# Weight copies and weight sums placed at other points of an attention and mixer kernel on one Trainium2 core, and one weight piece converted elsewhere

## The chip, the core and the metric

The kernel runs on one core of a Trainium2 chip. The metric is device time in microseconds, the median of the runs shown. Names of engines: PE (TensorE, matmuls; PEld its weight loads), DVE (VectorE), ACT (ScalarE), POOL (GpSimd), SP (SyncE, which here issues nearly all DMAs, in order).

## What is computed

Windowed attention over 8 batches, 8 heads, 576 positions and head size 64, and then a mixer block. From the reference:

```python
scores = scale * np.matmul(q, k.transpose(0, 1, 3, 2))
mask = (rel >= 0) & (rel < 64)                      # rel = query position - key position
attn = softmax(np.where(mask, scores, -1e9))
x = (attn @ v) as (batch 8, seq 576, channels 512)
xt = x.transpose(0, 2, 1)
h = np.maximum(xt @ w_tok1, 0.0) @ w_tok2           # (576, 256), (256, 576)
u = x + h.transpose(0, 2, 1)
h2 = np.maximum(u @ w_ch1, 0.0) @ w_ch2             # (512, 1536), (1536, 512)
out = u + h2
```

The activations are float32, the four weights float64.

## The kernel before

**Precision.** Each float32 operand of a large product is split into two parts, `hi` (ACT's copy) and `lo` (the difference, by DVE or POOL), and a product is three matmuls: hi with hi, hi with lo, lo with hi. The float64 weights arrive as pairs of 32-bit words. Turning 384 columns of them into float32 is a *job*. `to_f32_a` (L195 to L198) and `to_f32_b` (L207 to L212) are six operations on DVE, with the last addition on POOL during attention; for *late* jobs ACT makes the absolute value (L185) and DVE adds. Jobs 0 to 6 are the token weights, 7 to 22 are `w_ch1` (kept in SBUF as `w1hi`, `w1lo`), 23 to 38 are `w_ch2` (`w2hi`, `w2lo`).

**Attention.** 36 tiles of 128 query rows, numbered `i`. In a tile, PE transposes the softmax, forms the output `xp`, the scores two tiles ahead, and the token product `h`; in spare places it also makes pieces of `u`, which are stored to `u_dram`. `JOBS[i]` says how many jobs tile `i` converts: one, except that tiles from 6 on whose number divides by 3 convert none. A job that is converted in one tile is finished in the next: a `w1` job is split (ACT, POOL), a `w2` job is stored to `w2_dram`, since the memory of `w2hi` and `w2lo` is not free yet. `N_FIRST` = 27 jobs are done here, four of them `w2`.

**The channel product** runs over nine chunks of 512 tokens. Chunk 0 is done whole: 12 pieces `gemm1` (L620, 12 matmuls each, into `gp`), each followed by `relu_split` (L607 on ACT gives `ghi`, L608 on DVE gives `glo`), and then four `gemm2` (L628, 36 matmuls each, `op_0` to `op_3`), each followed by `add_out` (L633 on DVE, L635 the store). Beside chunk 0 run the late jobs (`late_steps`, two steps a piece), and the four `w2` jobs that had been stored are read back 512 columns at a time (`load_w2`, L571, tile `raww2`) and split (`split_w2`, L104). `op_0` needs columns 0 to 1535 of `w2`, `op_1` the next 1536, and so on. A `raw` tile has three buffers, so the load of a late job on SP waits until DVE has done the L210 of the third job before it.

Chunks 1 and 2 are done in halves: 6 pieces of `gemm1`, then four `gemm2` of 18 matmuls. Chunks 3 to 8 are done in pairs by a scheme with seven products (`m1` to `m7`) for eight, which needs sums and differences of blocks of `w1`. These are prepared during chunk 1. `weight_steps` is a generator: it copies the blocks that need no sum to DRAM (`w1s`), 12 DMAs, and then makes four rounds of four steps, each with sums on DVE (L689 to L711), a split (`keep`, L101 on ACT and L104 on DVE, tiles `whi` and `wlo` with four buffers each), and two stores by `store_w1`. Chunk 1 takes two steps per piece. During chunk 2, SP begins to load the blocks from `w1s` into the place of `w1hi` and `w1lo`.

**Order.** The order of instructions on each engine is the order in which the program writes them (the schedule is manual). Every engine takes its own in order; semaphores tie them together. SP waits in order too: a DMA whose condition isn't met holds all that are behind it.

Of the kernel before, what the change touches and what calls it, by code (L numbers as in the profile page):

```python
# [10 lines left out]
F32 = mybir.dt.float32  # L11
# [10 lines left out]
C = H * D  # L22
P = 128
# [7 lines left out]
NCT = C // P  # L31
# [5 lines left out]

LAST_PARTS = 2

N_FIRST = 27  # L40


JOBS = {i: 1 if i < 6 or i % 3 else 0 for i in range(-1, 37)}
PIECES = {32: (1, 0), 33: (1, 0), 34: (1, 0), 35: (3, 0), 36: (2, 1)}

TOK1_FROM, TOK1_SLOW, TOK2_FROM = 2, 4, 7
# [8 lines left out]
NH = NFT // 2  # L55
PRODUCTS = ("m1", "m6", "m7", "m5", "m2", "m4", "m3")
# [27 lines left out]
def mixer_kernel(ctx: ExitStack, tc: tile.TileContext, qh, kh, vh, wt1, wt2, wc1, wc2, out):  # L84
    nc = tc.nc
# [7 lines left out]
    w1hi = const.tile([P, NCT * F], F32R, name="w1hi")  # L93
    w1lo = const.tile([P, NCT * F], F32R, name="w1lo")
    w2_dram = dram.tile([P, NFT * C], F32, name="w2_dram")
    w1s = [dram.tile([P, NH, NPROD, 2, P], F32, name=f"w1s{k}") for k in range(2)]
    u_dram = [dram.tile([P, NCT, CHUNK], F32, name=f"u_dram{j}") for j in range(NCHUNK)]

    def split(eng_hi, eng_lo, hi, lo, src):
        if eng_hi is nc.scalar:  # L100
            nc.scalar.copy(hi, src)  # L101
        else:
            eng_hi.tensor_copy(hi, src)
        eng_lo.tensor_sub(lo, src, hi.bitcast(F32))  # L104
# [18 lines left out]
    with ExitStack() as actx:  # L123
# [92 lines left out]
        jobs = [(wt1, t1hi, t1lo, o, 320) for o in range(0, 5 * DT, 320)]  # L216
        jobs += [(wt2, t2hi, t2lo, o, CW) for o in range(0, NTT * S, CW)]
        jobs += [(wc1, w1hi, w1lo, o, CW) for o in range(0, NCT * F, CW)]
        jobs += [(wc2, None, None, o, CW) for o in range(0, NFT * C, CW)]
        to_load, to_convert, to_finish = list(range(N_FIRST)), [], []  # L220

# [10 lines left out]
        def job_convert_a():  # L232
            if to_convert:
                n, raw = to_convert.pop(0)
                to_convert_b.append((n, to_f32_a(raw, jobs[n][4], n, n >= N_FIRST)))

# [5 lines left out]
        finished = set()  # L242

        def job_finish():
            if to_finish:
# [5 lines left out]
                else:  # L251
                    eng = nc.vector if src is wt2 or n >= N_FIRST else nc.gpsimd
                    split(nc.scalar, eng, hi[:, o:o + m], lo[:, o:o + m], w)
# [212 lines left out]
        tok1_plan, n = {}, 0  # L466
        for i in range(TOK1_FROM, NT + 1):
            m = min(n + (1 if i < TOK1_SLOW else 2), i)
            tok1_plan[i] = range(n, m)
            n = m  # L470
        qk(0)
        for i in range(-1, NT + 1):
# [6 lines left out]
            store_u()  # L479
            n_jobs = JOBS[i]  # L480
            if i == NT - 1:
# [67 lines left out]
    with ExitStack() as bctx:  # L549
# [11 lines left out]
        tctx = ExitStack()  # L561
        pl = tctx.enter_context(tc.tile_pool(name="pl", bufs=1))
        cpool[0] = pl
        first = [(o, C) for o in range(0, jobs[N_FIRST][3], C)]
        w2_raw = []

        def load_w2():
# [6 lines left out]
        def split_w2():  # L574
            if w2_raw:
                o, m, raw = w2_raw.pop(0)
                split(nc.scalar, nc.vector, w2hf[:, o:o + m], w2lf[:, o:o + m], raw[:, :m])

        to_load += range(N_FIRST, len(jobs))
        for n in to_load:  # L580
# [51 lines left out]
        def add_out(j, uf, ct, op, final, cols=slice(0, CHUNK)):  # L632
            nc.vector.tensor_add(uf[:, ct, cols], op, uf[:, ct, cols])  # L633
            if final:
                nc.sync.dma_start(out[j, :, ct, cols], uf[:, ct, cols])  # L635
# [5 lines left out]
            return ps.tile([P, CHUNK], F32, name=f"op{name}_{ct}", tag=tag, bufs=bufs)  # L641


        u = ul.pop(0)
        for ft in range(NFT):
            gemm1(0, ft, u, gbuf[ft])
            for _ in range(2):
                next(late, None)
            if ft in (1, 2, 7):
                load_w2()  # L650
            if ft in (6, 8, 10):
                split_w2()
            if ft == 3:
                ul[1] = load_u(1, pu)
            if ft == 8:
                split_u(ul[1])
        for ct in range(NCT):
            for _ in range(7):
                next(late, None)
            assert all(n in finished for n in range(23 + 4 * ct, 27 + 4 * ct))  # L660
            op = new_op("0", ct)
            gemm2(op, ct, range(NFT), gbuf, True, True)
            add_out(0, u[0], ct, op, True)
        tctx.close()


        pw = tctx.enter_context(tc.tile_pool(name="pw", bufs=1, reuse_waits="tile"))

        def store_w1(m, k, f0, ct, src):

            nf = src.shape[1] // P
            nc.sync.dma_start(w1s[k][:, f0:f0 + nf, PRODUCTS.index(m), ct],  # L672
                              src.bitcast(F32).rearrange("p (f c) -> p f c", c=P))

        def weight_steps():
            for m, half, ct0 in (("m1", 0, 0), ("m2", 0, 2), ("m4", 1, 2)):
                for ct in range(2):
                    for k, w in enumerate((w1hi, w1lo)):
                        o = (half * NCT + ct0 + ct) * NH * P
                        store_w1(m, k, 0, ct, w[:, o:o + NH * P])  # L680
            yield
            nf = CW // P
            for n in range(2 * NH // nf):
                ct, f0 = n % 2, n // 2 * nf

                def whole(tag, half, ct):
                    o = (half * NCT + ct) * NH * P + f0 * P
                    t = pw.tile([P, CW], F32, name=f"{tag}_{n}", tag=tag, bufs=1)
                    nc.vector.tensor_add(t, w1hi[:, o:o + CW].bitcast(F32), w1lo[:, o:o + CW].bitcast(F32))  # L689
                    return t  # L690

                def keep(m, x):
                    hi, lo = (pw.tile([P, CW], F32R, name=f"w{k}_{m}_{n}", tag=f"w{k}", bufs=4) for k in ("hi", "lo"))
                    split(nc.scalar, nc.vector, hi, lo, x)
                    for k, t in enumerate((hi, lo)):
                        store_w1(m, k, f0, ct, t)

                a = whole("wa", 1, ct)
                s1 = whole("ws", 1, 2 + ct)
                yield  # L700
                nc.vector.tensor_add(s1, s1, a)
                c = whole("wb", 0, ct)
                keep("m5", s1)
                yield
                nc.vector.tensor_sub(a, c, a)
                nc.vector.tensor_sub(c, s1, c)
                keep("m7", a)
                keep("m6", c)
                yield
                d = whole("wd", 0, 2 + ct)  # L710
                nc.vector.tensor_sub(d, d, c)  # L711
                keep("m3", d)
                yield
# [40 lines left out]


        steps = weight_steps()
        for j in range(1, N_PLAIN):
            u, last = ul.pop(j), j == N_PLAIN - 1
            if last:
                tctx.close()  # L760
                px.append(bctx.enter_context(tc.tile_pool(name="px", bufs=1, reuse_waits="tile")))
                load_raw(0, 0)
            for half in range(2):
                g = []
                for ft in range(half * NH, (half + 1) * NH):
                    g.append(new_g(f"{j}_{ft}"))
                    gemm1(j, ft, u, g[-1])
                    if j == 1:
                        for _ in range(2):
                            next(steps, None)  # L770
                    if not last and ft == 3:
                        ul[j + 1] = load_u(j + 1, pu)
                    if not last and ft == 8:
                        split_u(ul[j + 1])
                    if last:
                        if ft == 1:
                            sums()
                            prep(0, "m1", 0)
                            prep(0, "m6", 0)
                        if ft == 2:  # L780
                            prep(0, "m7", 0)
                            prep(0, "m5", 0)
                            prep(0, "m2", 0)
                            load_raw(0, 1)
                        if ft == 6:
                            load_w1(0)
                            sums()
                        if ft in (7, 8):
                            for m in (("m1", "m6"), ("m7", "m5", "m2"))[ft - 7]:
                                prep(0, m, 1)  # L790
                        if ft == 9:
                            sum4()
                if last and half == 1:
                    for m in ("m4", "m3"):
                        prep(0, m, 1)
                    load_raw(0, 0)
                    load_w1(1)
                    load_w1(2)
                for ct in range(NCT):
                    op = new_op(f"{j}_{half}", ct)  # L800
                    gemm2(op, ct, range(half * NH, (half + 1) * NH), g, True, True)
                    add_out(j, u[0], ct, op, half == 1)
                    if last and half == 1 and ct == 1:
                        sums(False)
                        sum4()
                        for m in ("m4", "m3"):
                            prep(0, m, 0)
# [132 lines left out]
```

## Time and profile before

| | |
|---|---|
| median of 3 runs | 866.21 us (866.21 to 866.83) |
| the profiled execution | 867.31 us, of which its span is 865.5 us |
| PE busy | 828.6 us, 96% of the span |
| DVE busy | 527.3 us, 61% |
| ACT busy | 336.4 us, 39% |
| POOL busy | 104.8 us, 12%, in attention alone |
| DMA | 136.11 MB, mean 157 GB/s |

The stages in the profiled execution: attention to about 283 us, chunk 0 to 350.7, chunk 1 to 427.6, chunk 2 to 492.9, the three pairs to the end. PE is the engine to look at: where it is busy all the time at full clock, another engine's work costs nothing. So a stage is read by its length beside what its matmuls need.

### The profile page before, as it was taken

The page shows a single profiled execution, that of the slowest core. Times are in us where ns is not written, and L with a number is a line of the kernel's source. Part 1 is how long each engine was busy: PE and PEld are TensorE (multiplying, and loading weights), DVE is VectorE, ACT ScalarE, POOL GpSimd, SP SyncE. Part 2 cuts the span into 40 slices and gives each one's busy share as a digit, 9 for nine tenths or more (in the row PEclk, how much of TensorE's full clock was granted, in tenths as well). Part 3 has the DMA queues.
Part 4 walks back from the last instruction along what each step waited for, and adds up shares of the span by engine and source line. Part 5 has one row for each costly group of instructions (what it writes and reads, how often), then busy time and mean ns, then how long its engine had stood idle before and what let it go on. Part 6 is the DMA issues. An engine that isn't in the chain of part 4 may idle for free.

```text
span 865.5 us, 14815 instructions
## 1 busy us (share of the span) xinstructions
PE 828.6 (96%) x5864; PEld 680.8 (79%) x5864; DVE 527.3 (61%) x939; ACT 336.4 (39%) x1018; POOL 104.8 (12%) x109
## 2 busy tenths in 40 slices
PE   6889999989989999969999999999999999999998
PEld 4668878868879878848888888887888888888886
DVE  4989878878885598555244443447735367635252
ACT  4778778778786351122022120213211123202020
POOL 3533343333332000000000000000000000000000
PEclk9999999999999999979999999999999999999999
DMA  9657676666644542792240751606361424542002
GB/s 323 201 189 250 191 247 220 217 210 232 207 153 132 161 141 85 204 275 82 87 154 1 267 200 69 219 1 218 109 256 60 159 86 135 182 182 86 1 0 98
DMA packets 71334, 136.11 MB, mean 157 GB/s; under 512 B 7008, under 2 KB 41568, under 8 KB 69344
## 3 DMA queue, kind: packets, MB, share of 16 engines
q1 hardware_dynamic: 69152, 133.32, 45.9%
q10 hardware_dynamic: 2112, 1.84, 0.6%
q8 instruction: 46, 0.75, 0.4%
q14 instruction: 24, 0.20, 0.1%
HBM read 104.46 MB, written 30.67 MB: 156 GB/s over the span
## 4 chain that ended last, share of the span: by engine, by line
PE 77%; DVE 10%; ACT 4%; SPq 2%; issue 2%; POOL 2%; DMA 2%; POOLq 0%; DVEq 0%; ACTq 0%
PE gp L839 18%; PE op L628 11%; PE gp L620 6%; PE h L368 5%; PE up L410 4%; PE s L276 4%; PE op_4a L628 4%; PE op_2b L628 4%; PE op_2a L628 4%; PE op_0b L628 4%; PE op_0a L628 4%; PE op_4b L628 4%; PE xp L323 3%; PE up L403 2%; SPq L672 2%
## 5 line engine op out<-in xcount | busy, mean ns | idle before, releaser
L839 PE MATMUL gp<-m,w1hi 128*128 128x512 f32 x504 | 155.4, 389 | 0.7 <-DVE x L847 0.7
L839 PEld LDWEIGHTS gp<-m,w1hi 128*128 128x128 f32 x504 | 94.5, 188 | 20.9 <-DVE x L847 1.5
L839 PE MATMUL gp<-m,w1lo 128*128 128x512 f32 x252 | 98.0, 389 | 0.0
L304 ACT ACTIVATE e<-e,nm 128x128 f32<-128x128 f32 x232 | 90.4, 396 | 8.2 <-DVE nm L296 8.2
L607 ACT ACTIVATE ghi<-x 128x512 fp32r<-128x512 f32 x54 | 34.1, 632 | 119.9 <-DVE x L849 68.3
L843 ACT COPY x<-gp 128x512 f32<-128x512 f32 x18 | 10.4, 578 | 143.8 <-PE gp L839 143.8
L607 ACT ACTIVATE ghi<-gp 128x512 fp32r<-128x512 f32 x50 | 29.6, 595 | 82.7 <-PE gp L620 82.5
L608 DVE SCALAR_TENSOR_TENSOR glo<-x,ghi 128x512 fp32r<-128x512 f32 x54 | 37.4, 693 | 38.1 <-ACT ghi L607 38.1
L628 PE MATMUL op<-ghi,w2hi 128*128 128x512 f32 x128 | 51.4, 401 | 6.0 <-ACT ghi L607 6.0
L620 PE MATMUL gp<-ulo,w1hi 128*128 128x512 f32 x144 | 56.0, 389 | 0.0
L620 PE MATMUL gp<-uhi,w1hi 128*128 128x512 f32 x144 | 56.0, 389 | 0.0
L620 PE MATMUL gp<-uhi,w1lo 128*128 128x512 f32 x144 | 56.0, 389 | 0.0
L839 PEld LDWEIGHTS gp<-m,w1lo 128*128 128x128 f32 x252 | 47.3, 188 | 9.9
L628 PE MATMUL op<-glo,w2hi 128*128 128x512 f32 x128 | 51.3, 401 | 0.9 <-DVE glo L608 0.8
L628 PE MATMUL op<-ghi,w2lo 128*128 128x512 f32 x128 | 51.0, 398 | 0.0
L104 POOL TENSOR_TENSOR xlo<-x,xhi 128x512 fp32r<-128x512 f32 x32 | 42.6, 1332 | 65.2 <-ACT xhi L101 64.8
L323 PEld LDWEIGHTS xp<-v,pt 128*64 128x64 f32 x1152 | 37.4, 137 | 16.5 <-ACT pt L313 6.2
L608 DVE SCALAR_TENSOR_TENSOR glo<-gp,ghi 128x512 fp32r<-128x512 f32 x50 | 34.2, 686 | 25.8 <-ACT ghi L607 25.7
L276 PE MATMUL s<-k,q 64*64 64x128 f32 x1152 | 43.4, 287 | 3.4 <-DVE c L207 1.9
L323 PE MATMUL xp<-v,pt 128*64 128x64 f32 x1152 | 43.2, 226 | 2.6 <-ACT pt L313 2.2
L304 ACT ACTIVATION_READ_ACCUMULATOR e<-e,nm 128x1 f32 x232 | 44.7, 193 | 0.0
L313 ACT COPY pt<-pp 128x512 f32<-128x512 f32 x72 | 41.9, 586 | 6.6 <-PE pp L311 6.4
(165 smaller groups left out, 1894.6 us busy)
## 6 DMA issues: line engine op xcount, KB each, us to landing
v<-vh SPq DMA_DIRECT2D x36, 512.0 KB, 3.7
w1hi<-w1s SPq DMA_DIRECT2D x18, 896.0 KB, 4.8
w1lo<-w1s SPq DMA_DIRECT2D x18, 896.0 KB, 6.6
raw<-wc SPq DMA_DIRECT2D x32, 384.0 KB, 4.4
q<-qh SPq DMA_DIRECT2D x36, 256.0 KB, 4.5
k<-kh SPq DMA_DIRECT2D x7, 1280.0 KB, 7.6
out<-uf SPq DMA_DIRECT2D x35, 256.0 KB, 2.6
uf<-u_dram SPq DMA_DIRECT2D x8, 1024.0 KB, 8.7
```

The costliest lines, as they stand in the source:

```text
L104: eng_lo.tensor_sub(lo, src, hi.bitcast(F32))
L276: nc.tensor.matmul(s[u][half * BLK:(half + 1) * BLK, j], qt[r, j, half], kbs[b][r, j, n * BLK:n * BLK + P], start=not on_pe, stop=True, sk ...
L304: nc.scalar.activation(e[:, h], src[:, h], AF.Exp, bias=nm[:, g:g + 1], scale=by, accum_out=sm[:, g:g + 1])
L313: nc.scalar.copy(pt, pp)
L323: nc.tensor.matmul(xp[half * BLK:(half + 1) * BLK, h], pts[h % 2][:, h // 2, half * BLK:(half + 1) * BLK], vt[:, half, h], start=True, sto ...
L368: nc.tensor.matmul(h_ps[b][tt], w[:, o + tt * P:o + (tt + 1) * P], x, start=first and n == 0, stop=last and n == len(combos) - 1)
L410: nc.tensor.matmul(up[:, :n], hx[:, cs], w[:, tt * S + s0:tt * S + s0 + n], start=False, stop=(k == 6), skip_group_check=True)
L607: nc.scalar.activation(hi, src, AF.Relu)
L608: nc.vector.scalar_tensor_tensor(out=lo, in0=src, scalar=0.0, in1=hi.bitcast(F32), op0=ALU.max, op1=ALU.subtract)
L620: nc.tensor.matmul(gp, w[:, w1_at(ft, ct)], x[:, ct], start=(k == 0), stop=(k == 3 * NCT - 1))
L628: nc.tensor.matmul(op, w[:, ct, ft], x[:, cols], start=(first and k == 0), stop=(last and k == 3 * len(gs) - 1), skip_group_check=not (fir ...
L839: nc.tensor.matmul(b, w[:, at], c[:, h, t], start=(n < 4 and k == 0), stop=(k == 5), skip_group_check=True)
```

## The change

It does three things.

- `N_FIRST` is 28 and tile 21 converts a job as well. The jobs from 17 on move one place ahead among the converting tiles, a fifth `w2` job (number 27) is stored to `w2_dram`, and eleven late jobs are left. A fourth `load_w2` (384 columns) and a fourth `split_w2` read it back beside chunk 0, and the splits stand behind pieces 6, 8, 9 and 11 instead of 6, 8 and 10.
- The 12 copies of blocks of `w1` leave `weight_steps`. Three of them follow each `gemm2` and its `add_out` in chunk 0.
- Chunk 1 takes one step of `weight_steps` per piece of `gemm1` and one per `gemm2`.

```diff
-N_FIRST = 27
+N_FIRST = 28
-JOBS = {i: 1 if i < 6 or i % 3 else 0 for i in range(-1, 37)}
+JOBS = {i: 1 if i < 6 or i % 3 or i == 21 else 0 for i in range(-1, 37)}
...
-        first = [(o, C) for o in range(0, jobs[N_FIRST][3], C)]
+        first = [(o, min(C, jobs[N_FIRST][3] - o)) for o in range(0, jobs[N_FIRST][3], C)]
...
+        quarters = [(m, k, ct, (half * NCT + ct0 + ct) * NH * P) for m, half, ct0 in
+                    (("m1", 0, 0), ("m2", 0, 2), ("m4", 1, 2)) for ct in range(2) for k in range(2)]
...
-            if ft in (1, 2, 7):
+            if ft in (1, 2, 7, 9):
                 load_w2()
-            if ft in (6, 8, 10):
+            if ft in (6, 8, 9, 11):
                 split_w2()
...
             op = new_op("0", ct)
             gemm2(op, ct, range(NFT), gbuf, True, True)
             add_out(0, u[0], ct, op, True)
+            for m, k, t, o in quarters[3 * ct:3 * ct + 3]:
+                store_w1(m, k, 0, t, (w1hi, w1lo)[k][:, o:o + NH * P])
         tctx.close()
...
         def weight_steps():
-            for m, half, ct0 in (("m1", 0, 0), ("m2", 0, 2), ("m4", 1, 2)):
-                for ct in range(2):
-                    for k, w in enumerate((w1hi, w1lo)):
-                        o = (half * NCT + ct0 + ct) * NH * P
-                        store_w1(m, k, 0, ct, w[:, o:o + NH * P])
-            yield
...
                     gemm1(j, ft, u, g[-1])
                     if j == 1:
-                        for _ in range(2):
-                            next(steps, None)
+                        next(steps, None)
...
                     add_out(j, u[0], ct, op, half == 1)
+                    if j == 1:
+                        next(steps, None)
```

What moves, on three engines. In the rows, a number behind a name tells instances apart; `raw` is a late job's load, `raww` a read of converted `w2`.

On SP, from the third read of converted `w2` to the outputs of chunk 0 and the copies, before:

```order
L571 DMA raww_1024_4631<-w_dram 128x512
L227 DMA raw_4650<-wc 128x384
L227 DMA raw_4689<-wc 128x384
L227 DMA raw_4735<-wc 128x384
L227 DMA raw_4749<-wc 128x384
L635 DMA out<-uf_4246 128x512 x4
L672 DMA w1s_69<-w1hi 768x1x128
L672 DMA w1s_70<-w1lo 768x1x128
```

and with the change:

```order
L571 DMA raww_1024_4644<-w_dram 128x512
L227 DMA raw_4663<-wc 128x384
L227 DMA raw_4702<-wc 128x384
L571 DMA raww_1536_4704<-w_dram 128x384
L227 DMA raw_4750<-wc 128x384
L635 DMA out<-uf_4259 128x512
L647 DMA w1s_69<-w1hi 768x1x128
L647 DMA w1s_70<-w1lo 768x1x128
L647 DMA w1s_69<-w1hi 768x1x128
L635 DMA out<-uf_4259 128x512
```

One late load is gone, a read of 384 columns stands between the last two, and three copies follow each output instead of twelve behind the fourth.

On DVE, at the end of chunk 0's first products (`gp_10` and `gp_11` are its last two pieces), before:

```order
L198 TENSOR_SCALAR c_4685<-c_4685 128x384
L608 SCALAR_TENSOR_TENSOR glox<-gp_10_4691,ghix 128x512
L104 TENSOR_TENSOR w2lo<-w_4680,w2hi 128x384
L207 SCALAR_TENSOR_TENSOR c_4685<-raw_4573,c_4685 128x384
L209 TENSOR_SCALAR r_4708<-c_4685 128x384
L210 SCALAR_TENSOR_TENSOR r_4708<-raw_4573,r_4708 128x384
L212 TENSOR_TENSOR w_4709<-r_4708,c_4685 128x384
L104 TENSOR_TENSOR w2lo<-raww_1024_4631,w2hi 128x512
L608 SCALAR_TENSOR_TENSOR glox<-gp_11_4718,ghix 128x512
```

and with the change:

```order
L104 TENSOR_TENSOR w2lo<-raww_1024_4644,w2hi 128x512
L608 SCALAR_TENSOR_TENSOR glox<-gp_10_4708,ghix 128x512
L104 TENSOR_TENSOR w2lo<-w_4693,w2hi 128x384
L207 SCALAR_TENSOR_TENSOR c_4698<-raw_4586,c_4698 128x384
L209 TENSOR_SCALAR r_4725<-c_4698 128x384
L210 SCALAR_TENSOR_TENSOR r_4725<-raw_4586,r_4725 128x384
L212 TENSOR_TENSOR w_4726<-r_4725,c_4698 128x384
L608 SCALAR_TENSOR_TENSOR glox<-gp_11_4733,ghix 128x512
L197 TENSOR_SCALAR c_4731<-c_4731 128x384
L198 TENSOR_SCALAR c_4731<-c_4731 128x384
L104 TENSOR_TENSOR w2lo<-w_4726,w2hi 128x384
L104 TENSOR_TENSOR w2lo<-raww_1536_4704,w2hi 128x384
```

The third split moves ahead of `gp_10`'s `glox`, and a fourth stands four rows behind `gp_11`'s. SP's load `raw_4702` uses the buffer that the L210 on `raw_4586` reads last.

On DVE in chunk 1, from its second piece on (L701 to L711 are the sums, L104 the splits of `keep`), before:

```order
L608 SCALAR_TENSOR_TENSOR glo_1_4991<-gp_1_4992,ghi_1_4990 128x512
L701 TENSOR_TENSOR ws_4988<-ws_4988,wa_4986 128x384
L689 TENSOR_TENSOR wb_5008<-w1hi,w1lo 128x384
L104 TENSOR_TENSOR wlo_m_0_5011<-ws_4988,whi_m_0_5010 128x384
L705 TENSOR_TENSOR wa_4986<-wb_5008,wa_4986 128x384
L706 TENSOR_TENSOR wb_5008<-ws_4988,wb_5008 128x384
L104 TENSOR_TENSOR wlo_m_0_5019<-wa_4986,whi_m_0_5018 128x384
L104 TENSOR_TENSOR wlo_m_0_5025<-wb_5008,whi_m_0_5024 128x384
L608 SCALAR_TENSOR_TENSOR glo_2_5031<-gp_2_5032,ghi_2_5030 128x512
```

and with the change:

```order
L608 SCALAR_TENSOR_TENSOR glo_1_4994<-gp_1_4995,ghi_1_4993 128x512
L701 TENSOR_TENSOR ws_4991<-ws_4991,wa_4989 128x384
L689 TENSOR_TENSOR wb_5011<-w1hi,w1lo 128x384
L104 TENSOR_TENSOR wlo_m_0_5014<-ws_4991,whi_m_0_5013 128x384
L608 SCALAR_TENSOR_TENSOR glo_2_5020<-gp_2_5021,ghi_2_5019 128x512
L705 TENSOR_TENSOR wa_4989<-wb_5011,wa_4989 128x384
L706 TENSOR_TENSOR wb_5011<-ws_4991,wb_5011 128x384
L104 TENSOR_TENSOR wlo_m_0_5039<-wa_4989,whi_m_0_5038 128x384
L104 TENSOR_TENSOR wlo_m_0_5045<-wb_5011,whi_m_0_5044 128x384
L608 SCALAR_TENSOR_TENSOR glo_3_5051<-gp_3_5052,ghi_3_5050 128x512
```

One step now stands between two `glo`, where two stood.

More of the change, by code (lines that the diff above doesn't have):

```diff
@@ L641, in new_op, with store_w1 @@
             return ps.tile([P, CHUNK], F32, name=f"op{name}_{ct}", tag=tag, bufs=bufs)
+        def store_w1(m, k, f0, ct, src):
+            nf = src.shape[1] // P
+            nc.sync.dma_start(w1s[k][:, f0:f0 + nf, PRODUCTS.index(m), ct],
+                              src.bitcast(F32).rearrange("p (f c) -> p f c", c=P))
+        quarters = [(m, k, ct, (half * NCT + ct0 + ct) * NH * P) for m, half, ct0 in
+                    (("m1", 0, 0), ("m2", 0, 2), ("m4", 1, 2)) for ct in range(2) for k in range(2)]
         u = ul.pop(0)
@@ L659, in mixer_kernel @@
                 next(late, None)
-            assert all(n in finished for n in range(23 + 4 * ct, 27 + 4 * ct))
+            assert all(n in finished for n in range(len(jobs) - 16, len(jobs) - 12 + 4 * ct))
             op = new_op("0", ct)
@@ L663, in mixer_kernel @@
             add_out(0, u[0], ct, op, True)
+            for m, k, t, o in quarters[3 * ct:3 * ct + 3]:
+                store_w1(m, k, 0, t, (w1hi, w1lo)[k][:, o:o + NH * P])
         tctx.close()
         pw = tctx.enter_context(tc.tile_pool(name="pw", bufs=1, reuse_waits="tile"))
[L669 to L673, printed above, removed]
         def weight_steps():
-            for m, half, ct0 in (("m1", 0, 0), ("m2", 0, 2), ("m4", 1, 2)):
-                for ct in range(2):
-                    for k, w in enumerate((w1hi, w1lo)):
-                        o = (half * NCT + ct0 + ct) * NH * P
-                        store_w1(m, k, 0, ct, w[:, o:o + NH * P])
-            yield
             nf = CW // P
```

## The prediction

> **What bounds the kernel now.** I first read the chain of work that ended last, in order of time, to see where it leaves the matmuls:
>
> ```profile
> 323.83 27.07 PE op L628 x118
> 354.24 1.31 SPq L672
> ...
> 371.46 3.13 DMA w1s<-wlo_m
> 379.67 15.30 PE op L628 x56
> 394.97 16.32 PE gp L620 x72
> 411.29 16.32 PE op L628 x72
> ```
>
> Columns: start, duration, what. From 394.97 on the chain is matmuls almost without a break. Between 351 and 380 it runs through SP's queue, which issues the copies of `w1hi` and `w1lo` (L672), and through a store that lands. The last two rows also give a price: 72 matmuls of 512 columns take 16.32 us, 0.2267 us each from start to start.
>
> Second, the busy time by stage (stretch, length, then busy time and count of PE, PEld, DVE, ACT, POOL, then TensorE's granted clock, DMA share, GB/s). The rows are: first products of chunk 0, its second products, then the two halves of chunk 1, except that the last row is only the first products of the second half:
>
> ```profile
> 283.40:316.00 32.60, 32.60 (x145) 27.00 (x145) 24.28 (x51) 14.47 (x30) 0.00 (x0) 1.00 0.54 174
> 316.00:350.70 34.70, 32.96 (x145) 26.96 (x145) 25.81 (x56) 7.47 (x16) 0.00 (x0) 1.00 0.23 69
> 350.70:367.00 16.30, 16.30 (x73) 13.51 (x72) 11.31 (x21) 4.24 (x8) 0.00 (x0) 1.00 0.89 256
> 367.00:395.00 28.00, 21.07 (x74) 15.63 (x74) 12.04 (x22) 4.57 (x9) 0.00 (x0) 0.82 0.79 221
> 395.00:411.30 16.30, 16.30 (x73) 13.50 (x72) 12.05 (x22) 6.46 (x13) 0.00 (x0) 1.00 0.39 109
> ```
>
> Two rows are longer than their matmuls. The second products of chunk 0 take 34.70 us where 144 matmuls need 32.64, and those of chunk 1's first half take 28.00 where 72 need 16.32, with the clock down to 0.82. Who made PE wait in 280 to 500 us (us in total, times, longest):
>
> ```profile
> PE op L628 <- ACT ghi L607: 6.0, 2, 5.1
> PE op L628 <- DVE w2lo L104: 1.7, 1, 1.7
> PE op L628 <- DVE glo L608: 0.8, 1, 0.8
> ```
>
> Third, why `ghi` was late; the rows are ACT's, DVE's and PE's in order of time:
>
> ```profile
> 371.25 0.51 ACT L101 CAST whi_m<-ws 128x384 fp32r<-128x384 f32 x1 [6.90 <-DMA w1s<-whi_m]
> 374.41 0.59 ACT L607 ACTIVATE ghi<-gp 128x512 fp32r<-128x512 f32 x1
> ...
> 371.91 0.56 DVE L104 TENSOR_TENSOR wlo_m<-ws,whi_m 128x384 fp32r<-128x384 f32 x1 [5.00 <-DMA w1s<-wlo_m]
> ...
> 375.05 0.79 PE L628 MATMUL op<-ghi,w2hi 128*128 128x512 f32 x1 [5.13 <-ACT ghi L607]
> ```
>
> `keep` has four `whi` and four `wlo` buffers. The fifth needs the first one's store to have landed, and that store was queued behind twelve copies. ACT waited 6.90 us in a weight split, with the `ghi` that PE needed queued behind it.
>
> **The change, part by part.**
>
> *Copies.* They are 12 of 384 KB, 4.72 MB, in one burst before. What a burst moves:
>
> ```profile
> w1s<-w1hi SPq DMA_DIRECT2D x6, 384.0 KB, 5.1
> 361.00:371.00 10.00, 8.93 (x40) 7.06 (x38) 5.26 (x11) 1.53 (x4) 0.00 (x0) 1.00 1.00 287
> ```
>
> The DMA engines were full at 287 GB/s, so the burst needs 4.72 MB / 287 GB/s = 16.4 us. Now three copies stand behind each output of chunk 0. With its output of 256 KB, each group is 1.44 MB, 5.0 us. The stage has DMA share 0.23, so 27 of its 34.7 us are free. DVE adds an output only after late conversions that stand ahead of it, so I place the groups at about 337, 342, 345 and 354; the last is through at about 359, 5 us into chunk 1. The issues on SP hold only outputs and copies there, for which no engine waits. Cost: nothing, covered by matmuls; if that cover went, the last group's 5 us would stand ahead of chunk 1's stores.
>
> *Sums, one step at a time.* Sixteen steps now take 12 pieces of first product and 4 of the 8 second ones, instead of 17 calls within 9 pieces. A piece of 12 matmuls lasts 2.72 us. A round of four steps stores 8 x 192 KB = 1.57 MB, 5.5 us at 287 GB/s, in at least 10.9 us. The first reuse of a `whi` buffer comes in piece 5, about 16 us into chunk 1; the store it waits for is issued at about 8 us and lands some 5 us later, since the copies end at 5. ACT's next `ghi` is in front of that split in the order, so PE does not depend on it either. I take the stall as gone entirely: 28.00 less 16.32, with the edges of the chain (394.97 less 350.73 less 2 x 16.32), is **-11.6 us**. The 0.82 clock of that row is inside the figure.
>
> *The fourth read of converted `w2`.* This is the edit with a price. Around chunk 0's first `op`, PE, DVE and SP before:
>
> ```profile
> 321.71 0.39 PE L628 MATMUL op<-glox,w2hi 128*128 128x512 f32 x1
> 323.83 0.50 PE L628 MATMUL op<-ghix,w2lo 128*128 128x512 f32 x1 [1.74 <-DVE w2lo L104]
> ...
> 319.98 0.68 DVE L608 SCALAR_TENSOR_TENSOR glox<-gp,ghix 128x512 fp32r<-128x512 f32 x1
> 322.02 0.56 DVE L210 SCALAR_TENSOR_TENSOR r<-raw,r 128x384 f32<-128x384 uint32 x1
> 323.09 0.68 DVE L104 TENSOR_TENSOR w2lo<-raww,w2hi 128x512 fp32r<-128x512 f32 x1
> 323.69 0.68 DVE L608 SCALAR_TENSOR_TENSOR glox<-gp,ghix 128x512 fp32r<-128x512 f32 x1
> ...
> 322.64 7.90 SPq L227 DMA_DIRECT2D raw<-wc  x3
> ...
> raww<-w_dram SPq DMA_DIRECT2D x1, 256.0 KB, 3.7
> ```
>
> Unhindered, the matmul at 323.83 would have started at 321.71 + 0.23 = 321.94: 1.9 us of loss, 2.05 by the stage. The third `w2lo` split now stands ahead of `glox` 10, so it ends near 320.6 and that wait goes. `glox` 11 still starts at 323.69, with as many instructions ahead of it; its matmul would start at 323.75 and starts at about 324.4. Then `op_1` begins at 324.8, and needs the piece that the fourth read brings. On SP this read stands behind the raw load that waits for the L210 of 322.02, now 0.6 later (the split moved ahead): that load goes out at 323.2, the read at 323.6. A read right behind a raw load landed in 3.7 us; this one has 192 KB instead of 256, so I take 3.5 (3.0 to 4.0): 327.1. ACT's cast comes next, 0.5, then PE at 327.75 and the `w2lo` split in time for the third matmul within 0.1. Unhindered, `op_1` would start at 321.94 + 10 x 0.2267 = 324.2. The loss is 3.7 instead of 2.05: **+1.7 us** (+1.2 to +2.2). The cast and the split stand ahead of later conversions on ACT and DVE; those slip to about 341.5, and the last product that needs them starts at 344. One conversion less takes about 3 us off DVE there (six operations of some half a microsecond, as the L210), for a split of 0.5.
>
> *The clock behind that wait.* PE would idle 0.6 and then 2.9 us in 4 us. What the granted clock did after idling:
>
> ```profile
> 50.10:53.50 3.40, 1.16 (x24) 0.85 (x28) 3.26 (x9) 2.74 (x11) 0.00 (x0) 1.00 0.94 293
> 53.50:57.00 3.50, 3.50 (x37) 3.17 (x38) 3.43 (x6) 1.22 (x3) 2.27 (x2) 0.51 0.41 162
> ...
> 371.00:374.40 3.40, 0.00 (x0) 0.00 (x0) 2.14 (x4) 1.43 (x3) 0.00 (x0) 1.00 1.02 287
> 374.40:377.80 3.40, 2.01 (x3) 0.79 (x3) 2.46 (x5) 1.42 (x4) 0.00 (x0) 0.50 1.03 287
> ...
> 319.80:323.20 3.40, 2.29 (x11) 1.56 (x9) 3.30 (x8) 1.60 (x4) 0.00 (x0) 1.00 0.43 116
> ```
>
> A stretch of 3.4 us with 2.24 us of idling was followed by 0.51; one with 1.11 was not. An idle time of 2.9 puts over 2.2 into one such stretch for about three quarters of the positions it can have. Half speed for 3.4 us costs 1.7, less what falls into the wait: **+1.6 us** (0 to +3.0).
>
> [...]
>
> *The piece in attention tile 21.* It adds six DVE operations and a POOL addition there, and an ACT copy and a POOL subtraction a tile later; from there each tile converts the next number, and tile 30 loses one such copy and subtraction for a store.
>
> ```profile
> 165.90:171.00 5.10, 5.10 (x83) 4.35 (x82) 3.58 (x7) 3.48 (x17) 0.91 (x1) 1.00 0.42 124
> L198 DVE TENSOR_SCALAR c<-c 128x384 int32<-128x384 int32 x14 | 12.4, 885 | 0.5
> L210 DVE SCALAR_TENSOR_TENSOR r<-raw,r 128x384 f32<-128x384 uint32 x13 | 7.3, 559 | 0.5
> PE h L368 <- POOL xlo L104: 2.5, 6, 0.9
> ```
>
> Six operations of 0.3 to 0.9 us are about 3 us; DVE has 5.10 - 3.58 = 1.5 us free in that tile, and more behind it. PE's longest wait for POOL's `xlo`, in 60 to 260 us, is 0.9. I take **+0.3 us** (-0.3 to +1.0), nearest to the tiles with a conversion, where PE stays nearly full.
>
> *Sum.* The profiled execution took 867.31 us (span 865.5), 1.10 above the median of 866.21. 867.31 - 11.6 + 1.7 + 1.6 + 0.3 = 859.3; less 1.1 it is **858.2 us** for the median.
>
> **The rivals.**
>
> A, the forecast: the stall in chunk 1 goes, a new wait for the fourth read stands at `op_1`, and the clock falls behind it. 858.2, its own range 857.0 to 860.0.
>
> B: as A, but the clock stays up, because the position of the stretches spares it, or because only full ones count. 866.2 - 11.6 + 1.7 + 0.3 = 856.6. The row at 50.10 speaks against the second reason. [...]
>
> C: the read lands before `op_1` needs it. Then `op_1`'s third matmul waits only for the `w2lo` split, at 324.3 plus 0.35 + 0.36 and two splits of 0.5, less overlaps, 326.0 instead of 324.65: 1.4 of loss instead of 2.05, and 866.2 - 11.6 - 0.65 + 0.3 = 854.3. Against it: SP is one queue, and the row at 322.64 is a load that waited for DVE.
>
> D: the copies end later than I place them and one `whi` wait remains ahead of a `ghi`: one landing, 3 us, and the clock's 1.6. 862.8. Against it: some 8 us of slack.
>
> E, the other side: the read lands so late that its wait eats the gain. The gain besides it is 11.3 us, and before 2.05 of loss stood there already; with a clock at half behind it, a landing from about 335 on, 8 us later than I reckon, decides. At 340 it would be 871. For it: the read's place behind a blocked load. Against it: no read of this kind took over 4 us.
>
> **How the numbers follow.** A 0.45, B 0.24, C 0.14, D 0.12, E 0.05. The likeliest is A, 858.2. The range takes in B, C and part of the way to D: 854.0 to 861.2 leaves out D's upper part and E, and somewhat of C. What this kernel's runs can tell from no change is about 0.2%, 1.7 us: all of A to D lie beyond 864.5 on the fast side, but D could grow; so faster 0.94, same 0.02, slower 0.04.
>
> **What would show it.** Right: in the profile after, PE's wait for `ghi` at `op_0` of chunk 1 is gone, and each half of chunk 1 takes 32.6 us; the copies are issued between 335 and 357; PE waits 2.5 to 3.3 us for ACT's or DVE's `w2` at the start of `op_1`, and the granted clock is 0.5 for some 3.4 us behind it. No such wait shows C right; one of over 8 us E. A remaining wait of `whi` for a store ahead of a `ghi` shows D. The tiles from 21 on should begin at most 1 us later. Wrong it would be if the read's issue does not follow the DVE operation that I tie it to, or if a store or output on SP holds something that I take for covered.

## The result, and the profile after

The changed kernel takes 860.59 us (median of four runs, 859.85 to 861.71), the kernel before 866.52 us beside it (four runs, 866.21 to 868.95). The ratio is 0.9927, its interval 0.9904 to 0.9949: faster by 0.7%. The forecast was 858.2, its range 854.0 to 861.2. The sign and the case (A) came true; the time is 2.4 us above the forecast, 0.6 us beyond A's own range (857.0 to 860.0) and inside the whole range.

The profiled execution of after took 861.26 us, its span 859.5. First its chain of work that ended last (start, duration, what), which answers to the first rows shown of before:

```profile
325.46 0.33 SPq L227
...
325.84 3.49 DMA raww<-w_dram
...
329.36 0.52 ACT w2hi L101
...
329.92 26.50 PE op L628 x108
356.42 16.32 PE gp L620 x72
372.74 16.32 PE op L628 x72
389.06 16.32 PE gp L620 x72
405.38 16.32 PE op L628 x72
```

From 356.42 on, chunk 1 is matmuls without a break: two halves of 32.64 us. SP's copies and the store that landed, which held the chain from 351 to 380 in before, are gone. In front of them stands what was forecast: the raw load on SP, the fourth read (3.49 us), ACT's cast of it, then `op_1`.

Who made PE wait in 280 to 500 us (total, times, longest):

```profile
PE op L628 <- ACT w2hi L101: 2.5, 1, 2.5
PE op L628 <- DVE glox L608: 0.4, 1, 0.4
```

And the busy time around that wait, cut where the granted clock changes (stretch, length, busy time and count of PE, PEld, DVE, ACT, POOL, then clock, DMA share, GB/s):

```profile
324.05:327.46 3.41, 2.96 (x12) 1.80 (x10) 3.27 (x8) 0.51 (x1) 0.00 (x0) 1.00 0.27 52
327.46:330.87 3.41, 0.95 (x4) 0.61 (x5) 1.23 (x3) 0.96 (x2) 0.00 (x0) 1.00 0.31 121
330.87:334.28 3.41, 3.41 (x10) 2.67 (x9) 3.24 (x9) 0.99 (x2) 0.00 (x0) 0.50 0.37 93
```

A stretch with 0.95 us of matmuls, then one at half clock with 10 matmuls, where 3.41 / 0.2267 = 15 have room.

By stages, each counted from the start of its first matmul, in the two profiled executions (us; the chain above dates a row from the end of the matmul before it, 0.16 later):

```
                              before    after   difference
attention, to chunk 0's start 283.38   285.74      +2.36
chunk 0                        67.35    70.52      +3.17
chunk 1                        76.72    65.28     -11.44
the rest                      438.07   437.95      -0.12
```

The differences add up to -6.0, as the spans do. Chunk 1 and chunk 0 came out to 0.2 us as the sum had them (-11.6, and +1.7 + 1.6). Attention, with +0.3 in the sum, is the term that was missed.

### The profile page after: what moved, and what is told of

Same layout as the page of the kernel before. It is cut to its first block, busy times and chain, and to the rows that moved or that the text cites. A ratio compares the mean times of both kernels' runs of the same rounds, so it can differ in the third digit from the quotient of the medians.

```text
span 859.5 us, 14823 instructions
## 1 busy us (share of the span) xinstructions
PE 829.2 (96%) x5864; PEld 682.4 (79%) x5864; DVE 530.2 (62%) x939; ACT 336.6 (39%) x1017; POOL 105.6 (12%) x110
## 3 DMA queue, kind: packets, MB, share of 16 engines
q10 hardware_dynamic: 2112, 1.84, 0.6%
## 4 chain that ended last, share of the span: by engine, by line
PE 77%; DVE 14%; ACT 4%; issue 2%; POOL 2%; DMA 2%; POOLq 0%; SPq 0%; DVEq 0%; ACTq 0%
PE gp L840 18%; PE op L628 11%; PE gp L620 8%; PE h L368 4%; PE op_4a L628 4%; PE op_2b L628 4%; PE op_2a L628 4%; PE op_0a L628 4%; PE op_0b L628 4%; PE op_4b L628 4%; PE up L410 4%; PE s L276 4%; PE xp L323 3%; PE up L403 2%; POOL xlo L104 2%
## 5 line engine op out<-in xcount | busy, mean ns | idle before, releaser
L104 POOL TENSOR_TENSOR xlo<-x,xhi 128x512 fp32r<-128x512 f32 x32 | 42.6, 1331 | 62.8 <-ACT xhi L101 62.4
```

## The experiments

Beside the first four kernels the kernel before had a median of 867.79 us (7 runs), beside the other four 867.43 (10 runs). Lengths of stages are those of each profiled execution, counted as in the table above.

**Copies and sums spread, without the additional piece.** Edit, against after:

```diff
-N_FIRST = 28
+N_FIRST = 27
-JOBS = {i: 1 if i < 6 or i % 3 or i == 21 else 0 for i in range(-1, 37)}
+JOBS = {i: 1 if i < 6 or i % 3 else 0 for i in range(-1, 37)}
...
-            if ft in (1, 2, 7, 9):
+            if ft in (1, 2, 7):
...
-            if ft in (6, 8, 9, 11):
+            if ft in (6, 8, 10):
```

> The copies and sums of the change alone: 27 pieces in attention, twelve late, splits behind pieces 6, 8 and 10 as before. Theory 1 (the gain is chunk 1's stall; the piece in tile 21 and the fourth read only cost): chunk 1 takes 65.3 us, chunk 0 67.3 as before, attention as before; 11.6 below the kernel before, about 854.8, faster than the whole change by about 6. Theory 2 (the room that the moved piece makes beside chunk 0 is needed for the copies; without it the late jobs and copies get in each other's way): chunk 0 longer than 67.3 or a wait left in chunk 1, about 858 to 861. Theory 3 (attention's 2 to 3 us more in the change's profile were chance between executions): this run is only about 3 us below the whole change.

Measured: 856.13 us, ratio 0.987 (0.9853 to 0.9887). Attention takes 282.59, chunk 0 67.45, chunk 1 65.28. So the spreading brings all of the gain, and the additional piece costs 4 to 5 us of it.

**The additional piece alone**, in the kernel before:

```diff
-N_FIRST = 27
+N_FIRST = 28
-JOBS = {i: 1 if i < 6 or i % 3 else 0 for i in range(-1, 37)}
+JOBS = {i: 1 if i < 6 or i % 3 or i == 21 else 0 for i in range(-1, 37)}
...
-        first = [(o, C) for o in range(0, jobs[N_FIRST][3], C)]
+        first = [(o, min(C, jobs[N_FIRST][3] - o)) for o in range(0, jobs[N_FIRST][3], C)]
...
-            if ft in (1, 2, 7):
+            if ft in (1, 2, 7, 9):
...
-            if ft in (6, 8, 10):
+            if ft in (6, 8, 9, 11):
...
```

> The piece in tile 21 and the fourth read alone; copies and sums as before. Theory 1: chunk 1 keeps its stall of 11.6, chunk 0 takes 1.7 to 3.4 more, attention 1.2 to 3 more: 869.5 to 872.5. Theory 2: some gain in chunk 1 from the piece, so below 866. Theory 3: attention as before, 868 to 870.

Measured: 872.48 us, ratio 1.0057 (1.0039 to 1.0075): slower. Tiles 23 and 24 of attention take 18.55 us instead of 15.55, chunk 0 70.72 and chunk 1 76.0. Its waits of PE in 280 to 500 us:

```profile
PE op L628 <- ACT ghi L607: 6.1, 2, 5.1
PE op L628 <- ACT w2hi L101: 2.6, 1, 2.6
PE op L628 <- DVE glo L608: 0.8, 1, 0.8
PE op L628 <- DVE glox L608: 0.5, 1, 0.5
```

The old wait for `ghi` is untouched, and the new one for the read stands beside it. The two parts add: the piece alone costs 4.7 us, about what it takes from the spreading's gain in the change.

**The fourth read one piece earlier.** Edit, against after: `load_w2()` is issued behind the split of piece 8, ahead of the raw load that SP waits with.

```diff
-            if ft in (1, 2, 7, 9):
+            if ft in (1, 2, 7):
...
+            if ft == 8:
+                load_w2()
```

> The whole change, but the fourth read is issued behind piece 8 instead of 9, so that on SP it stands in front of the late load that waits for DVE. Theory 1 (the wait at op_1 is the late landing of that read): the read goes out near 319 in the time of before, PE's wait for ACT's w2hi at op_1 is gone, what is left is 1.3 to 1.5 of waiting for DVE, no half clock there; chunk 0 takes 66.6 to 67 instead of 70.7; about 857. Rival (ACT and DVE are late anyway, the read is not the cause): chunk 0 stays at 69 or more, 859 to 861.

Measured: 856.34 us, ratio 0.9869 (0.9853 to 0.9886). Chunk 0 is 66.80 instead of 70.52, the granted clock stays at 1.00 there (in the stretches from 321.00 to 334.30 us), and this is all that is left of its waits:

```profile
PE op L628 <- DVE glox L608: 0.5, 1, 0.5
PE op L628 <- DVE w2lo L104: 0.4, 1, 0.4
```

Both terms of the forecast's +3.3 are shown by it: the wait was the read's place behind the blocked load, and the clock, 0.50 behind the wait in after, did not fall without it. Attention (285.48) did not change; it is another cost.

**The third split one piece earlier, without the additional piece.** Edit, against the first experiment:

```diff
-            if ft in (6, 8, 10):
+            if ft in (6, 8, 9):
```

> As e1, with the third split behind piece 9 instead of 10, as the whole change has it. Theory 1: the wait of 1.7 for w2lo in op_0 shrinks to about 0.6 for the last glo, and op_1 needs no read that is late: chunk 0 takes 66.0 to 66.3 instead of 67.3, about 853.6. Rival (DVE is so full there that the wait only moves to the last glo or to op_3, whose pieces are done at about 342): chunk 0 stays at 67, about 854.8.

Measured: 854.46 us, ratio 0.9849 (0.9835 to 0.9864): the lowest median here, below both kernels. Its four runs (854.07 to 854.92) lie below all four of the first experiment (855.23 to 857.70), though the intervals of the two ratios overlap. Chunk 0 is 65.99; the wait for `w2lo` (1.8 us in the first experiment) is gone:

```profile
PE op L628 <- DVE glox L608: 0.4, 1, 0.4
```

**Only the copies moved**, sums at two steps a piece as before (27 pieces ahead). Edit, against the first experiment:

```diff
                     if j == 1:
-                        next(steps, None)
+                        for _ in range(2):
+                            next(steps, None)
...
-                    if j == 1:
-                        next(steps, None)
```

> 27 pieces ahead, as before, and the sums as before (two steps in each piece of first product of chunk 1, none in the second products); only the copies of w1hi and w1lo are moved, three behind each output of chunk 0. Theory 1 (the burst of twelve copies in front of the sums' stores is what held the whi buffer, so moving it is enough): PE's wait of 5.1 us for ghi in chunk 1 goes, chunk 1 takes 65.3 us as in the run with copies and sums spread, 855 to 857 us. Theory 2 (the sums' own pace is the cause as well: four steps store 1.57 MB, 5.5 us at 287 GB/s, in two pieces of 2.7 us): a whi split still waits 2 to 4 us for a store ahead of a ghi, chunk 1 takes 68 to 74 us, 859 to 864 us.

Measured: 863.21 us, ratio 0.9949 (0.9934 to 0.9964), chunk 1 72.57. Theory 1 falls: moving the burst away recovers only 4.2 of the 11.4 us. Theory 2 had the right size, but not the reason, since no split waits for a store any more. ACT in this kernel (the cast of each sum and `ghi`, with the idle time before and who ended it; "issue" stands where the view names nobody, and DVE's L701 had just ended there, at 365.03):

```profile
356.74 0.51 ACT L101 CAST whi_m<-ws 128x384 fp32r<-128x384 f32 x1 [2.34 <-DVE ws L701]
...
361.77 0.51 ACT L101 CAST whi_m<-wd 128x384 fp32r<-128x384 f32 x1 [1.69 <-DVE wd L711]
362.19 0.59 ACT L607 ACTIVATE ghi<-gp 128x512 fp32r<-128x512 f32 x1
365.11 0.51 ACT L101 CAST whi_m<-ws 128x384 fp32r<-128x384 f32 x1 [2.33 <-issue]
...
373.98 0.59 ACT L607 ACTIVATE ghi<-gp 128x512 fp32r<-128x512 f32 x1
```

and the busy time in one round of four steps, and then in the second products:

```profile
356.74:365.11 8.37, 8.37 (x39) 6.93 (x38) 7.49 (x15) 3.05 (x7) 0.00 (x0) 1.00 0.75 214
367.31:390.92 23.61, 20.25 (x73) 15.34 (x73) 12.75 (x23) 4.58 (x9) 0.00 (x0) 0.86 0.56 169
```

One round of four steps takes 365.11 - 356.74 = 8.37 us, while its two pieces of matmuls need 5.44. DVE alone has 12 operations of 0.55 and two `glo` of 0.69 in a round. That is 8.0 us end to end, and 7.49 us of busy time, since they overlap by some hundredths; most of the rest of the round it waits for ACT's casts. So the last `ghi` is made at 373.98, 6.7 us after the pieces end, and PE waits; the granted clock is 0.86 in that stage.

**Only the sums' steps spread**, with the burst of twelve copies where it was. Edit, against before:

```diff
                     if j == 1:
-                        for _ in range(2):
-                            next(steps, None)
+                        next(steps, None)
...
+                    if j == 1:
+                        next(steps, None)
```

> 27 pieces ahead and the twelve copies in one burst at the start of chunk 1, as before; only the sums' steps are spread, one in each piece of first product and one in each of the second. Theory 1: the burst needs 16.4 us and drains by about 20 us into chunk 1; the fifth whi split comes in the fifth piece, 13.6 to 16 us in, and waits some 5 us for its buffer, but what of ghi stands behind it decides: at a pace of one step a piece, the next ghi that PE needs is made after 16.3 us, so a wait of 2 to 5 us remains, chunk 1 takes 68 to 73 us, 859 to 863 us. Theory 2 (the pace of the sums alone is the cause): no wait for ghi, chunk 1 takes 65.3 us, 855 to 857 us.

Measured: 856.04 us, ratio 0.9873 (0.9851 to 0.9894), chunk 1 65.28: as good as both together. SP's last copy and the first store behind the burst:

```profile
364.95 1.34 SPq L672 DMA_DIRECT2D w1s<-w1lo  x1
366.39 1.29 SPq L672 DMA_DIRECT2D w1s<-whi_m  x1
```

ACT's last `ghi` of the first half and the fifth `whi`, and DVE's `wlo` of it:

```profile
367.15 0.59 ACT L607 ACTIVATE ghi<-gp 128x512 fp32r<-128x512 f32 x1
372.25 0.51 ACT L101 CAST whi_m<-ws 128x384 fp32r<-128x384 f32 x1 [4.50 <-DVE ws L701]
...
373.19 0.56 DVE L104 TENSOR_TENSOR wlo_m<-ws,whi_m 128x384 fp32r<-128x384 f32 x1 [0.55 <-DMA w1s<-wlo_m]
```

and the second products of the first half:

```profile
366.89:383.21 16.32, 16.32 (x74) 13.52 (x73) 9.42 (x17) 2.91 (x6) 0.00 (x0) 1.00 1.01 288
```

The burst holds the stores just as before, and DMA is full (share 1.01, 288 GB/s). But at one step a piece the fifth `whi` comes only behind the last `ghi` of the half, so that nothing PE needs is behind what waits. The pace decides; the copies' place does not, once the pace is right.

**The piece in tile 27 instead of 21.** Edit, against after:

```diff
-JOBS = {i: 1 if i < 6 or i % 3 or i == 21 else 0 for i in range(-1, 37)}
+JOBS = {i: 1 if i < 6 or i % 3 or i == 27 else 0 for i in range(-1, 37)}
```

> The changed kernel with the additional piece in attention tile 27 instead of tile 21. Theory 1 (the six DVE operations fill DVE so far that its operations meet POOL's and are stretched, until x of the third tile behind is late): the loss moves with the piece; tiles 22 to 24 are as before (15.7 us, not 17.25), and tiles 28 to 31 lengthen by 1 to 3 us in all, with a wait of PE for xhi or xlo of over 1 us and perhaps a granted clock of 0.5 behind it; 859 to 861 us. Theory 2 (only the place around tile 21 is so full, the added work by itself fits): attention is at most 0.5 us longer than before, 857.5 to 858.5 us. In both the wait at op_1 stays at about 2.5 us.

Measured: 859.44 us, ratio 0.9908 (0.9892 to 0.9924), whose interval overlaps that of after; what tells the two apart are the tiles. The time from one tile's first `xp` to the next one's, in the profiled executions (us; "spread only" is the first experiment, "w1lo on DVE" the next one; tile 25 is 7.1 in all):

```
tile   before  spread only  after  piece in 27  w1lo on DVE
22      7.27      7.27       7.26      7.28        7.14
23      8.43      8.44       9.99      8.41        9.67
24      7.12      7.13       8.56      7.12        7.13
26      7.28      7.31       7.29      7.54        7.30
27      7.36      7.34       7.35      7.61        7.35
28      7.06      7.06       7.09      7.44        7.06
29      7.00      6.97       6.98      7.41        6.98
```

The loss goes with the piece, as theory 1 has it. It is 1.3 us there, spread over tiles 26 to 29, and the clock stays up (1.00 in every stretch from 205 to 235 us); the wait of over 1 us that it expected did not show (the longest for `xlo` from 200 to 245 us is 0.4).

**`w1lo` of four pieces on DVE instead of POOL.** Edit, against after:

```diff
-                    eng = nc.vector if src is wt2 or n >= N_FIRST else nc.gpsimd
+                    eng = nc.vector if src is wt2 or n >= N_FIRST or n in (16, 17, 18, 19) else nc.gpsimd
```

> The changed kernel with the subtraction that makes w1lo done on DVE instead of POOL for four pieces of weights, numbers 16 to 19, around attention tiles 20 to 25. Theory 1 (DVE's plain TENSOR_SCALARs last as long as a POOL operation that runs beside them, 0.8 to 1.4 us instead of 0.16 to 0.36): fewer of them are stretched, which saves DVE up to 0.7 us for each, more than the 0.55 us that the subtraction adds; tiles 22 to 24 take 15.7 to 16.5 us instead of 17.25, 857.5 to 859.5 us. Theory 2 (DVE is simply too full with six operations more): four times 0.55 us more on DVE makes x later still; tiles 22 to 24 take 17.5 to 19 us, 861 to 863 us.

Measured: 861.22 us, ratio 0.9922 (0.9903 to 0.9941), not to be told from after. DVE and POOL in after, around tiles 21 to 23:

```profile
172.71 1.00 DVE L195 TENSOR_SCALAR c<-raw 128x384 int32<-128x384 int32 x1
180.19 1.39 DVE L195 TENSOR_SCALAR c<-raw 128x384 int32<-128x384 int32 x1
181.61 1.04 DVE L197 TENSOR_SCALAR c<-c 128x384 f32<-128x384 f32 x1
```

```profile
172.48 1.02 POOL L104 TENSOR_TENSOR w1lo<-w,w1hi 128x384 fp32r<-128x384 f32 x1
180.08 1.28 POOL L349 TENSOR_TENSOR xlo<-x,xlo 64x512 fp32r<-64x512 f32 x1
181.44 1.00 POOL L104 TENSOR_TENSOR w1lo<-w,w1hi 128x384 fp32r<-128x384 f32 x1
```

and DVE in the experiment:

```profile
173.00 0.35 DVE L195 TENSOR_SCALAR c<-raw 128x384 int32<-128x384 int32 x1
...
180.20 1.37 DVE L104 TENSOR_TENSOR w1lo<-w,w1hi 128x384 fp32r<-128x384 f32 x1 [0.15 <-ACT w1hi L101]
181.49 0.35 DVE L195 TENSOR_SCALAR c<-raw 128x384 int32<-128x384 int32 x1
181.87 0.36 DVE L197 TENSOR_SCALAR c<-c 128x384 f32<-128x384 f32 x1
```

What theory 1 says shows in these rows: the three on DVE in after begin while a POOL operation runs and end 0.21 to 0.22 us after it, and without one they take 0.35 and 0.36 us. But the subtraction itself takes 0.51 on DVE, and 1.37 where it meets POOL, so only 0.3 us of tile 23's 1.55 is won. Tiles 22 and 23 take 16.81 us instead of 17.25, between the two expectations; the time of the runs is theory 2's. That DVE is too full for the work, wherever `w1lo` is made, is the likely reading; no run shows it by itself, since the edit puts the subtraction on DVE in place of the meetings with POOL that it takes away.

## Why the prediction was right, and where it was not

**The stall in chunk 1: right in size, half right in its reason.** -11.6 was forecast, -11.44 measured; 0.16 of the difference is in the working, which took 394.97, a row of the chain, less 350.73, the start of a matmul (by starts it is 394.81). The working put it down to the store "queued behind twelve copies". The experiments with one part each show that two things were wrong at once, and that the pace of the sums is the one that counts: at two steps a piece DVE is busy for 7.5 us beside 5.44 us of matmuls, and 7.3 us are lost with no burst at all; at one step the burst costs nothing. The step that was lacking is a count of DVE's work in a round; the durations for it stood in the profile of before.

**The copies: right.** They go out from 339.9 to 358.9, which is 337.5 to 356.5 when the 2.36 us by which chunk 0 starts later are taken off (forecast: 335 to 357), and they cost nothing beside chunk 0. They bring nothing either: 856.13 with them moved and 856.04 without.

**The fourth read: right.** Take off the same 2.36 us: the read goes out at 325.84 - 2.36 = 323.5 (forecast 323.6), lands in 3.49 us (3.5), and `op_1` starts at 329.92 - 2.36 = 327.6 (327.75). What the forecast did not ask is whether the read could have gone out one row earlier on SP. It could, and that is worth 3.7 us of chunk 0.

**The clock behind it: right.** 1.6 us was forecast for it and 1.7 for the wait, and chunk 0 grew by 3.17. The rows give 1.6 for each: `op_1`'s fourth matmul starts at 330.85, 3.6 us later than unhindered (2.05 were lost before), and the nine matmuls from there take 3.65 us instead of 2.04. The second reason of rival B, that only full stretches count, did not hold: the stretch from 327.46 had 0.95 us of matmuls in it, and the clock was 0.50 in the next.

**The piece in tile 21: wrong, and this is the miss.** The sum had +0.3 (-0.3 to +1.0). Measured: tile 23 +1.55 and tile 24 +1.44, 3.0 in all, of which an earlier start of attention gave 0.6 back in this execution. The step that failed is "Six operations of 0.3 to 0.9 us are about 3 us; DVE has 5.10 - 3.58 = 1.5 us free in that tile, and more behind it". The room was there; the work was twice as large. From 165 us on, where tile 21's job begins in after, to the first `hlo` of tile 23, in the kernel with the spread alone and then in after:

```profile
165.02:182.68 17.66, 15.54 (x211) 12.60 (x212) 11.88 (x27) 13.76 (x53) 7.01 (x6) 0.97 0.60 188
165.26:184.28 19.02, 16.60 (x243) 13.61 (x246) 18.29 (x32) 14.83 (x54) 8.61 (x8) 1.00 0.74 222
```

The third busy time is DVE's (the clock of 0.97 is a fall at 181.5 that only that execution has there; tile 23 takes no longer for it). It grew by 6.4 us, not 3. The room: with the spread alone DVE waited for other engines 5.3 us in this stretch, in five waits. What the forecast left out is that the work pushes DVE's operations beside POOL's. Six TENSOR_SCALAR rows that run free of POOL elsewhere (0.16 to 0.36 us each, 1.6 in all) last 0.81 to 1.39 here, 6.1 in all; three of them are shown above. The backlog runs into tile 23, where two `hlo` stand behind it:

```profile
182.68 1.29 DVE L380 SCALAR_TENSOR_TENSOR hlo<-h,hhi 128x512 fp32r<-128x512 f32 x2 [2.57 <-ACT hhi L379]
```

```profile
184.28 1.28 DVE L380 SCALAR_TENSOR_TENSOR hlo<-h,hhi 128x512 fp32r<-128x512 f32 x2
```

With the spread alone DVE waited 2.57 us for this operation; in after it comes 1.60 us later and waits for nothing. DVE's `x` (L337) behind it comes 1.59 later, at 187.00 instead of 185.41, and PE waits for the two parts made of it:

```profile
188.39 0.50 PE L368 MATMUL h<-xhi,t1hi 128*128 128x512 f32 x1 [0.72 <-ACT xhi L101]
189.74 0.50 PE L368 MATMUL h<-xlo,t1hi 128*128 128x512 f32 x1 [0.85 <-POOL xlo L104]
```

The wait for `xhi` stands in neither of the two kernels without the piece, the one for `xlo` stood in before as well. Counted from the tile's own start, `x` comes 1.48 later than in both of them, and that is tile 23's 1.55. In the experiment with `w1lo` on DVE it comes 0.24 earlier within the tile than in after, and the tile is 0.3 shorter. No run keeps the piece and lets the six rows run free of POOL, so how much of the loss would be left without these meetings stays open.

Tile 24's 1.44 is the clock: three of the four profiled executions with the piece in tile 21 show it at half there for 3.4 us (0.50 from 190.92 to 194.33 in after; 1.98 us instead of 1.15 for the tile's 32 `xp` matmuls in all three), and the fourth (`w1lo` on DVE, 1.00 from 160 to 195 us) has neither the fall nor the loss. That this fourth is chance of position is likely, not shown: it is the fastest of its four runs (859.20), with one fall and a mean clock of 0.998, and the other three (860.83 to 861.71) have 0.994, as the profiled execution of after has with three falls.

**What was luck.** The total came within the range although this term was off by 2.1 us. The range reached to 861.2 to take in a part of the way to D, not because of attention. Two of the four runs of after (859.92 and 859.85) have a mean clock of 0.996, as if one of the three falls were lacking, and lie in A's own range; the other two, with 0.994, do not.

**Rivals.** B and C were not what happened: the wait for the read stood at `op_1` and the clock fell behind it. The experiment with the earlier read made C's case by hand, and it gave 856.3 (C's price was 854.3), with the loss in attention inside. D and E did not come: no `whi` wait stands ahead of a `ghi` that PE waited for, and the read landed at 329.3.

## What to carry to other kernels

Before a stall is put down to the transfer that ends it, count what each engine must do in one round of the loop and set it beside the round's matmuls: here that count, not the burst, decided. Price added work as it runs beside the other engines, not as it runs alone: here 3 us of it became 6.4. What does not fit into an engine's idle time costs where the backlog meets the first operation that PE waits for, here 1.55 us in tile 23. And on a queue that takes its transfers in order, as SP's did in these runs, look at what a read stands behind: one row made 3.7 us.

## What the hardware showed that was not expected

In after, each of the 40 TENSOR_SCALAR operations on DVE that begin while a TENSOR_TENSOR runs on POOL ends 0.02 to 0.26 us after it: 1.00 us instead of 0.35 beside `w1lo` (172.48 to 173.50 on POOL), 1.04 instead of 0.36. In the experiment with `w1lo` on DVE, a subtraction of two SBUF tensors takes 1.37 beside POOL's `xlo` instead of 0.51. In after, SCALAR_TENSOR_TENSOR from PSUM (L293) and TENSOR_REDUCE (L296) kept their 0.68 and 0.69 beside POOL. Why these differ, no run here shows.

The falls of the clock in these two profiles lie on a grid: in after they last 3.41 us each, at 0.50, and begin at 54.39, 190.92 and 330.87 us, 40 and 41 times 3.413 us apart, and the two of before begin at 53.54 and 374.39, 94 times that apart, and last 3.41 and 10.24 us. Stretches of that grid in after:

```profile
177.27:180.68 3.41, 1.84 (x14) 1.49 (x13) 3.34 (x7) 3.26 (x9) 2.86 (x3) 1.00 1.02 344
180.68:184.10 3.42, 2.65 (x55) 1.84 (x56) 3.32 (x5) 2.70 (x11) 1.68 (x2) 1.00 0.98 276
...
187.51:190.92 3.41, 1.84 (x7) 1.04 (x6) 3.31 (x7) 3.20 (x12) 2.90 (x3) 1.00 0.23 86
190.92:194.33 3.41, 3.41 (x58) 3.02 (x60) 0.99 (x2) 2.15 (x10) 0.00 (x0) 0.50 0.03 10
```

Of two stretches with PE busy for 1.84 us, the one was followed by full clock and the other by half. So 1.57 us of idle time (3.41 - 1.84) was enough once, less than the 2.2 that the forecast reckoned with, and these two show that the busy time alone does not tell when; what else counts stays open.
